# Opening order of a fused attention and MLP kernel: loads, normalization and small weights moved

## Chip, cores and metric

One core of one Trainium2 chip. The metric is the device time of one launch in microseconds, the median of several runs. The core has engines that run side by side, each with its own instruction stream in a fixed order: TensorE (PE, with weight loads shown as PEld), VectorE (DVE), ScalarE (ACT), GpSimd (POOL), and SyncE (SP), which here issues every DMA.

## What is computed

Sequence 2048, width 1024, 32 heads of 32, MLP width 3584, all in bf16.

```python
def reference(A_x, A_wqkv, A_wo, B_x, B_w1, B_b1, B_w2, B_b2):
    def _A_ref(x, wqkv, wo):
        qkv = (x @ wqkv).reshape(B, S, 3, H, Dh).transpose(2, 0, 3, 1, 4)
        q, k, v = qkv[0], qkv[1], qkv[2]
        scores = jnp.einsum("bhqd,bhkd->bhqk", q, k) * (Dh ** -0.5)
        o = jnp.einsum("bhqk,bhkd->bhqd", _softmax(scores, axis=-1), v)
        return o.transpose(0, 2, 1, 3).reshape(B, S, D) @ wo
    def _B_ref(x, w1, b1, w2, b2):
        y = _layernorm(x, axis=-1)
        return _gelu(y @ w1 + b1) @ w2 + b2
    x = A_x
    xn = _layernorm(x, axis=-1)
    s = _A_ref(xn, A_wqkv, A_wo)
    g = _silu(_B_ref(xn, B_w1, B_b1, B_w2, B_b2))
    return x + s * g
```

## The kernel before

x is cut into 16 tiles of 128 rows, t0 to t15. In the opening each tile is loaded, its mean and variance are taken (`bn_stats`, two halves of 512 columns on DVE; for t1 and t3 two activations with a running sum on ACT), the reciprocal root is made on POOL by a power, and DVE writes the normalized tile into one of four buffers `xnb` (L798). Then it is transposed into `xnT`: t0 to t3 and t5 by PE, with ACT copying the result out of PSUM (L786), the others by a DMA transpose on SP (L802), which waits for DVE.

Attention goes by head groups of four heads (eight groups), query blocks of 256 rows and pairs of key blocks. One *unit* is one head group, one query block, one block of 256 keys: eight score products on PE (L904), two exponentials of 128x1024 on ACT (L913). There are 512 units' worth of them. The K, Q and V projections of a head group must be there before its units; for the first group they are made in the opening, block by block (`k_item`, `q_item`, `v_half`), as tiles come in. K for blocks 0 to 2 is copied out of PSUM by ACT, from block 3 on by DVE. The first units go in the order `order0`: query blocks 0 and 1 on key blocks 0, 1, 2, ... with some of query block 2 between.

Between the scores PE does everything else: P times V, row sums, the projections of the next head group, and the MLP (W1 products in 112 items of 16, W2 products, L632). The W1 weights pass through three buffers `w1r`, the W2 weights through four `w2r`; in the opening the same memory holds exponentials of the first units, so the first W1 loads have to wait until these are used up. The MLP's input is x once more, normalized with another factor (`make_y`), transposed by DMA into `yT`.

In the last head group the output projection follows (L632 on `wo`, products of 512 columns): for the last query block seven of eight head groups can be summed ahead (`most`), and the eighth follows when the last quotient is there.

Who runs when is fixed when the program is built. A planner (`_Plan`) holds a list of operations with assumed durations (`occ`), latencies (`lat`), transfer rates and priorities (`prio`, smaller first), plays them through, and writes down one order for each engine. PE's items have positions and due units; `lead` is how many units ahead a due item gets precedence, `seeds` shake the positions in stretches of 30 us of the planner's time. `extra` names operations that a DMA must wait for beyond its data. So a changed constant can move instructions anywhere behind it. On the chip each engine goes through its order and waits at semaphores; nothing overtakes.

SP's order in the opening before: x0 to x3, wqk for K and Q, x4 to x11, the transpose of t4, x12, x13, wv, x14, x15, the other ten transposes, wqk for the next group's K, two loads of x for the MLP, b1, b2, wqk for its Q, two transposes for the MLP, then three W1 loads.

Of the kernel before, what the change touches and what calls it, by code (L numbers as in the profile page):

```python
# [8 lines left out]
BF16 = mybir.dt.bfloat16  # L9
# [23 lines left out]
class _Plan:  # L33
# [3 lines left out]
    def __init__(self):  # L37
        self.ops = []
        self.last_w = {}
        self.readers = {}  # L40
        self.s_queue = []
        self.pv_queue = []
        self.dense = {"pro": [], "q0": [], "v0": [], "tr": [], "last": [], "proj": [], "mlp": [], "w2": [], "wo": []}
        self.lead = 3
        self.filler, self.fill, self.fill0 = None, 0.6, 1400.0
        self.seeds, self.seg, self.amp, self.jit, self.w2b = (), 30000.0, 4.0, 0.1, 20.0
# [421 lines left out]
def bass_recurrent_scan__mha_block__mixer_channel_mlp__prompt_kernel(  # L468
# [27 lines left out]
        0, 0, 234914347, 0, 0, 0, 0, 0, 0, 0, 0, 0, 0, 0, 0, 0, 0, 0, 0, 0, 0, 0, 0, 0, 0, 0, 0, 0, 0,  # L496
# [3 lines left out]
    with ExitStack() as st:  # L500
# [28 lines left out]
        b1T = sb("b1T", [128, FB], BF16)  # L529
# [32 lines left out]
        xnb = [gw[:, i * 1024:(i + 1) * 1024] for i in range(4)]  # L562
        iota_i = utw[:].rearrange("p a b -> p (a b)")[:, 0:256].bitcast(I32)
# [19 lines left out]
        def c_b4(n):  # L583
            return 67 + 0.2605 * n
# [55 lines left out]
        def load_x(t, extra=()):  # L640
            dma(f"x{t}", lambda e: e.dma_start(xst[t], x2[t * 128:(t + 1) * 128, :]), 262144, [], [XS(t)],
                rate=390.0, prio=2, occ=500, lat=2450, extra=extra)
# [18 lines left out]
        for t in range(NTR, 12):  # L661
            load_x(t)
# [81 lines left out]
        def k_item(n):  # L744
            it = _Item("pro", 0.01 * n)
            for lo, w in ((0, 128), (128, 128)) if n < 2 else ((0, 256),):
                for dc in range(DC):
                    def fn(e, b, dc=dc, lo=lo, w=w):
                        at = n * 256 + lo
                        return mm(e, bank(b, lo, lo + w), wqk[wk0][:, dc, :], xnT[:, dc, at:at + w], dc == 0 and lo == 0, dc == DC - 1)  # L750
                    chunk(it, fn, Q256 if w == 256 else Q128, [("xnT", 2 * n + i, dc) for i in range(lo // 128, (lo + w) // 128)] + [("wqk", wk0)])
            if n >= 3:
                dve(lambda e: e.tensor_copy(QKT[0][:, 1, n * 256:(n + 1) * 256], bank(it.bank, 0, 256)), c_ps(256), [],
                    [("K", 0, n)], -1, it)
                return it
            act(lambda e: e.activation(QKT[0][:, 1, n * 256:(n + 1) * 256], bank(it.bank, 0, 256), ACT.Copy), c_act(256), [],
                [("K", 0, n)], -1, it)
            return it
# [35 lines left out]
        first = {}  # L794

        def normalize(t, rs):
            def nf(e):
                return e.tensor_scalar(xnb[t % 4], xst[t], mv[:, t, 0:1], lnp[:, t, 1:2], op0=ALU.subtract, op1=ALU.mult)  # L798
            rw = ([XS(t), ("mv", t), rs], [("xnb", t % 4)], 1)
            first[t] = pool(nf, 1150, *rw) if t in PN else dve(nf, c_b4(1024) + 118, *rw)  # L800
            if t >= NTR and t not in TRP:
                dma(f"tr{t}", lambda e: e.dma_start_transpose(xnT[:, :, t * 128:(t + 1) * 128], xnb[t % 4]), 262144,  # L802
                    [("xnb", t % 4)], [("xnT", t, c) for c in range(DC)], prio=0, rate=300.0, occ=1300, lat={4: 2800, 6: 2400, 7: 2000}.get(t, 1000))
# [10 lines left out]
        for n in range(NPR):  # L814
            if n == 6:
                for t in range(12, NT):
                    load_x(t, [first[4]])
                    if t == 13:
                        load_v(0, [first[4]])
            groups = [(2 * n,), (2 * n + 1,)] if n < 2 else [(2 * n, 2 * n + 1)]  # L820
            for ts in groups:
# [13 lines left out]
                for t in ts:  # L835
                    if t in AT:
                        continue
                    for c in range(2):
                        dve(lambda e, t=t, c=c: e.bn_stats(stats[:, t, c, :], xst[t][:, c * 512:(c + 1) * 512]),  # L839
                            605, [XS(t)], [("st", t, c)], 1.2)  # L840
# [4 lines left out]
                if ts[0] not in AT:  # L845
                    dve(lambda e, lo=lo, hi=hi: e.tensor_scalar_add(lnp[:, lo:hi, 0], mv[:, lo:hi, 1], EPS), 80,
# [22 lines left out]
        for n in range(NPR // 2):  # L869
            plan.dense["v0"].append(v_half(0, n, "pro", 0.2 + 0.01 * n))  # L870
            plan.dense["v0"][-1].hold = 6 + 2 * n

        rss = [("rs", t) for t in range(4)] + [("rs", 2 * n) for n in range(2, NPR)]
# [7 lines left out]
        dma("b1", lambda e: e.dma_start(b1T[:], B_b1.rearrange("(fb p) -> p fb", p=128)), 8192, [("s3",)], [("b1",)], lat=5500)  # L881
        dma("b2", lambda e: e.dma_start(b2b[:], B_b2.rearrange("(o d) -> o d", o=1).to_broadcast([128, D])), 262144,
            [("s3",)], [("b2",)], occ=2900)
# [139 lines left out]
        def proj(hg, w):  # L1023
            wk = load_qk(hg, 1, [first[NT - 1]] if hg == 1 else ())
            wq = load_qk(hg, 0)
# [26 lines left out]
        def load_w1(p):  # L1052
            gi, pi = p % NW1R, p % NW1
            src = B_w1[:, pi * 256:(pi + 1) * 256].rearrange("(c p) f -> p c f", p=128)
            dma(f"w1{gi}", lambda e: e.dma_start(w1r[:, gi], src), 524288, [], [("w1", gi)], lat=3100.0)
# [9 lines left out]
        def make_y(c):  # L1065
            for t2 in range(2):
                t = 2 * c + t2
                dma(f"yx{t2}", lambda e, t=t, t2=t2: e.dma_start(yst_t[t2][:], x2[t * 128:(t + 1) * 128, :]), 262144, [],
                    [("yst", t2)], rate=390.0, extra=[w1_ev[4]] if c == 1 else ())
# [118 lines left out]
        def mlp(u0, u1):  # L1188
# [4 lines left out]
            for s_ in seq:  # L1193
# [5 lines left out]
                if s_[0] == "w1":  # L1199
                    load_w1(s_[1] * NW1 + s_[2])  # L1200
                    it = w1_item(s_[1], s_[2])
                else:
# [364 lines left out]
```

## Time and profile before

| | us |
|---|---|
| three runs | 1029.39, 1031.92, 1032.52 (median 1031.92) |
| the profiled execution | 1031.42 |
| its span in the profile | 1029.6 |
| ACT busy | 1016.6 |
| PE busy | 1004.2 |
| DVE busy | 956.8 |
| ACT idle in 0 to 50 us, all of it | 6.1 |
| ACT idle from 50 to 1000 us | 0.3 |
| ACT idle in the last 29.6 us | 6.6 |

The span is the profile's own clock, from the first to the last event; the profiled execution's time is 1.8 us more. PE's busy time counts overlapping matmuls by modelled ends and says little about how near PE is to its peak. The granted TensorE clock is full (1.00 in every window, 0.96 in the last). An engine's idle row names the engine or DMA whose event ended it.

### The profile page before, as it was taken

To read this page: it belongs to the slowest core of one execution; us is meant where nothing else is said; L and a number is where in the kernel's file an instruction comes from. 1 tells how busy PE (TensorE), PEld (TensorE's weight loads), DVE (VectorE), ACT (ScalarE), POOL (GpSimd) and SP (SyncE) were. 2 spreads that over 40 slices of the span, in tenths; PEclk is the share of its full clock that TensorE was granted. 3 is DMA by queue.
4 is the path that set the end of the run, shared out by engine and by line. 5 is a ranking of instruction groups with operands and counts; after the bars stand their busy time and mean duration, and the time that the engine had idled before them with its cause. 6 is when DMAs were issued, how large, how long until landed. Compare 5 with 4: busy or idle time off the path is not lost.

```text
span 1029.6 us, 31985 instructions
## 1 busy us (share of the span) xinstructions
PE 1004.2 (98%) x14355; PEld 635.9 (62%) x14355; DVE 956.8 (93%) x1365; ACT 1016.6 (99%) x1087; POOL 11.8 (1%) x21
## 2 busy tenths in 40 slices
PE   8999999999999999999999999999999999999997
PEld 7566656666766576666665676665666665564443
DVE  8899999899899998998899999998999889978987
ACT  8999999999999999999999999999999999999997
POOL 2200000000000000000000000000000000000000
PEclk9999999999999999999999999999999999999999
DMA  8867845745764767446556575556355753873331
GB/s 221 153 154 201 206 123 167 207 110 136 206 187 129 196 189 201 129 134 195 142 146 190 154 215 159 158 173 174 88 150 166 218 161 88 274 230 120 108 93 64
DMA packets 317146, 167.77 MB, mean 163 GB/s; under 512 B 55632, under 2 KB 304976, under 8 KB 317008
## 3 DMA queue, kind: packets, MB, share of 16 engines
q1 hardware_dynamic: 317008, 165.71, 58.2%
q8 instruction: 113, 1.85, 0.8%
q14 instruction: 25, 0.20, 0.1%
HBM read 146.55 MB, written 12.06 MB: 154 GB/s over the span
## 4 chain that ended last, share of the span: by engine, by line
ACT 78%; PE 10%; DVE 7%; DMA 4%; issue 1%; POOL 0%; SPq 0%
ACT P L913 71%; PE ps L632 7%; ACT ut L1127 4%; DMA w2r<-in_B_w_dram 3%; PE ps L904 2%; DVE stats L839 1%; PE ps L627 1%; ACT P L1248 1%; DVE PA L930 1%; ACT gw L1155 1%; DVE PR L944 1%; DMA xnT<-gw 1%; DVE gw L798 1%; ACT w2r L913 1%; DMA hT<-in_A_x_dram 0%
## 5 line engine op out<-in xcount | busy, mean ns | idle before, releaser
L913 ACT ACTIVATE P<-ps 128x1024 bf16<-128x1024 f32 x988 | 921.3, 1228 | 0.8 <-PE ps L904 0.7
L930 DVE TENSOR_TENSOR PA<-P 128x2048 bf16<-128x2048 bf16 x173 | 210.0, 1217 | 28.4 <-ACT P L913 27.7
L632 PE MATMUL ps<-yT,w1r 128*128 128x256 bf16 x1792 | 227.7, 273 | 0.4 <-DVE QKT L730 0.3
L632 PE MATMUL ps<-w2r,hT 128*128 128x256 bf16 x1792 | 223.8, 273 | 2.0 <-DMA w2r<-in_B_w_dram 1.2
L944 DVE TENSOR_TENSOR PR<-PR,PA 128x2048 bf16<-128x2048 bf16 x173 | 209.7, 1213 | 1.4
L904 PE MATMUL ps<-QKT 32*128 32x256 bf16 x4032 | 200.2, 273 | 8.7 <-ACT P L913 6.2
L632 PEld LDWEIGHTS ps<-yT,w1r 128*128 128x128 bf16 x1792 | 163.8, 98 | 53.1 <-issue 29.1
L632 PEld LDWEIGHTS ps<-w2r,hT 128*128 128x128 bf16 x1792 | 163.0, 98 | 52.4 <-issue 30.6
L904 PEld LDWEIGHTS ps<-QKT 32*128 32x128 bf16 x4032 | 59.7, 92 | 138.2 <-ACT P L913 130.0
L627 PE MATMUL ps<-P,V 128*32 128x256 bf16 (+1 forms) x4080 | 137.6, 272 | 0.0
L632 PE MATMUL ps<-xnT,wqk 128*128 128x512 bf16 (+2 forms) x584 | 132.2, 354 | 2.4 <-DMA xnT<-gw 1.0
L627 PEld LDWEIGHTS ps<-P,V 128*32 128x32 bf16 x4080 | 95.3, 96 | 33.2 <-issue 24.0
L632 PE MATMUL ps<-wv,xnT 128*128 128x256 bf16 (+2 forms) x704 | 87.8, 264 | 1.6 <-DMA xnT<-gw 1.0
L632 PEld LDWEIGHTS ps<-xnT,wqk 128*128 128x128 bf16 x584 | 49.9, 98 | 51.7 <-issue 15.2
L1096 DVE TENSOR_TENSOR hT<-ps,b1T 128x512 bf16<-128x512 f32 x112 | 76.8, 685 | 4.4 <-PE ps L632 4.0
L930 DVE TENSOR_TENSOR PR<-P 128x2048 bf16<-128x2048 bf16 x60 | 72.8, 1214 | 0.0
L632 PEld LDWEIGHTS ps<-wv,xnT 128*128 128x128 bf16 x704 | 55.8, 98 | 23.9 <-issue 10.8
L1127 ACT ACTIVATE ut<-ut 128x3072 bf16<-128x3072 bf16 (+2 forms) x27 | 59.6, 2206 | 0.0
L730 DVE CAST QKT<-ps 128x512 bf16<-128x512 f32 x58 | 39.7, 685 | 1.5 <-PE ps L632 1.1
L999 DVE STREAM_TRANSPOSE nt<-ps 128x256 f32<-128x256 f32 x63 | 27.9, 444 | 14.0 <-PE ps L627 13.9
L1121 DVE TENSOR_TENSOR ut<-hT 128x2048 bf16<-128x2048 bf16 (+1 forms) x37 | 35.3, 957 | 0.1
L1130 DVE TENSOR_TENSOR hT<-ut,hT 128x2048 bf16<-128x2048 bf16 (+1 forms) x37 | 35.0, 951 | 0.0
(116 smaller groups left out, 587.8 us busy)
## 6 DMA issues: line engine op xcount, KB each, us to landing
w1r<-in_B_w_dram SPq DMA_DIRECT2D x112, 512.0 KB, 4.4
w2r<-in_B_w_dram SPq DMA_DIRECT2D x128, 448.0 KB, 4.5
yst<-in_A_x_dram SPq DMA_DIRECT2D x18, 256.0 KB, 4.5
wqk<-in_A_wqkv_dram SPq DMA_DIRECT2D x16, 256.0 KB, 3.7
g_scratch<-gw SPq DMA_DIRECT2D x32, 128.0 KB, 3.3
hT<-in_A_x_dram SPq DMA_DIRECT2D x14, 256.0 KB, 3.9
o_scratch<-ot SPq DMA_DIRECT2D x56, 64.0 KB, 3.4
xnT<-o_scratch SPq DMA_DIRECT2D x7, 512.0 KB, 6.4
```

The costliest lines, as they stand in the source:

```text
L627: ins = e.matmul(dst(j), lhsT=lhsT(j), rhs=rhs(j), start=start, stop=stop, tile_position=(0, 32 * j), skip_group_check=True)
L632: return e.matmul(dst, lhsT=lhsT, rhs=rhs, start=start, stop=stop, skip_group_check=True)
L730: dve(lambda e: e.tensor_copy(QKT[sl][:, which, tq * 512:(tq + 1) * 512], bank(it.bank)), c_ps(512), [], [(nm, sl, 2 * tq), (nm, sl, 2 * t ...
L904: ins = e.matmul(bank(b0[j], kk * 256, (kk + 1) * 256), lhsT=QKT[sl][32 * j:32 * j + 32, 1, kb * 128:(kb + 1) * 128], rhs=QKT[sl][32 * j:3 ...
L913: x = act(lambda e, h=h: e.activation(Pt[pi][:, 2 * h:2 * h + 2].rearrange("p j k q -> p (j k q)"), ps[:, pr[h] * 1024:(pr[h] + 1) * 1024] ...
L930: return dve(lambda e: e.tensor_tensor(dst[:].rearrange("p u j q -> p (u j) q"), src[:].rearrange("p u j k q -> p (u j) k q")[:, :, 0, :], ...
L944: return dve(lambda e: e.tensor_tensor(fl3(pr), fl3(pr), fl3(PA[i]), op=ALU.add), c_b16(2048), [("PA", i), tok], [tok], 3.2)
L999: dve(lambda e: e.transpose(nt_t[:], bank(pv.bank, 256, 512)), c_ps(256) + 120, [], [("nt",)], prio, pv)
L1096: w1_ev[p] = dve(lambda e: e.tensor_tensor(hT[:, hs], bank(it.bank).rearrange("p (k t) -> p k t", k=2), b1T[:, 2 * pi:2 * pi + 2].unsqueez ...
L1121: dve(lambda e, u_=u_, x_=x_: e.tensor_tensor(u_, x_, x_, op=ALU.mult), c_b16(n), hs_, [("ut", ui)], gp)
L1127: act(lambda e: e.activation(ua, ua, ACT.Tanh, scale=GC), c_acts(run * 512), uts, uts, ga)
L1130: dve(lambda e, u_=u_, x_=x_: e.tensor_tensor(x_, u_, x_, op=ALU.mult), c_b16(n), [("ut", ui)] + hs_, hs_, gp)
```

## The change

- x loads: wv now goes out between x9 and x10. x12 and x13 wait for t4's normalization, x14 and x15 for t7's (before, all four and wv stood behind t4's).
- b1 is no longer loaded transposed in one DMA of single elements, but as four DMAs of 28 rows of 32 values into the tail of `ut`, early in the queue; GpSimd clears the place first, and DVE transposes it into `b1T` after the last normalization.
- K's third block is copied by DVE and not by ACT (`n >= 2`).
- The normalizations of t0 to t3 get precedence over statistics (priority 0.8 for 1).
- Later loads get conditions: wqk for the next group's K after t15's transpose, its Q after an exponential of the third query block, W1 loads 1 and 2 after such exponentials, the first x load for the MLP after t15's transpose, b2 after the fifth W1 item, wqk of group 2 after the third.
- Planner constants: `lead` 5 for 3, the one nonzero seed is 0, some assumed rates and durations. They issue nothing themselves, but move the order: in ACT's stream the first 12 and the last 101 of 1085 instructions stay in place, in PE's the first 55 and the last 3 of some 14,360.

```diff
-        self.lead = 3
+        self.lead = 5
...
-        0, 0, 234914347, 0, 0, 0, 0, 0, 0, 0, 0, 0, 0, 0, 0, 0, 0, 0, 0, 0, 0, 0, 0, 0, 0, 0, 0, 0, 0,
+        0, 0, 0, 0, 0, 0, 0, 0, 0, 0, 0, 0, 0, 0, 0, 0, 0, 0, 0, 0, 0, 0, 0, 0, 0, 0, 0, 0, 0,
...
-        b1T = sb("b1T", [128, FB], BF16)
+        b1T = sb("b1T", [128, 32], BF16)
...
+        b1c = utw[:, 7, 480:512]
...
-        for t in range(NTR, 12):
-            load_x(t)
+        load_x(4)
...
+        load_x(9)
+        load_v(0)
+        load_x(10)
+        load_x(11)
+        pool(lambda e: e.memset(b1c, 0.0), 150, [], [("b1c", k) for k in range(4)], 0)
+        for k in range(4):
+            dma(f"b1{k}", lambda e, k=k: e.dma_start(b1c[32 * k:32 * k + FB, :], B_b1.rearrange("(q b p) -> b q p", b=4, p=32)[k]),
+                2048, [], [("b1c", k)], prio=2)
...
-            if n >= 3:
+            if n >= 2:
                 dve(lambda e: e.tensor_copy(QKT[0][:, 1, n * 256:(n + 1) * 256], bank(it.bank, 0, 256)), c_ps(256), [],
...
-            rw = ([XS(t), ("mv", t), rs], [("xnb", t % 4)], 1)
+            rw = ([XS(t), ("mv", t), rs], [("xnb", t % 4)], 0.8 if t < NTR else 1)
...
-            if n == 6:
-                for t in range(12, NT):
-                    load_x(t, [first[4]])
-                    if t == 13:
-                        load_v(0, [first[4]])
+            if n == 3:
+                load_x(12, [first[4]])
+                load_x(13, [first[4]])
+            if n == 4:
+                load_x(14, [first[7]])
+                load_x(15, [first[7]])
...
+        dve(lambda e: e.transpose(b1T[:], b1c), c_b16(32) + 60, [("b1c", k) for k in range(4)], [("b1",), ("ut", 1)], 2.5, None, [first[NT - 1]])
...
-        dma("b1", lambda e: e.dma_start(b1T[:], B_b1.rearrange("(fb p) -> p fb", p=128)), 8192, [("s3",)], [("b1",)], lat=5500)
-        dma("b2", lambda e: e.dma_start(b2b[:], B_b2.rearrange("(o d) -> o d", o=1).to_broadcast([128, D])), 262144,
-            [("s3",)], [("b2",)], occ=2900)
...
-            wk = load_qk(hg, 1, [first[NT - 1]] if hg == 1 else ())
-            wq = load_qk(hg, 0)
+            wk = load_qk(hg, 1, [trs[NT - 1]] if hg == 1 else [w1_ev[2]] if hg == 2 else ())
+            wq = load_qk(hg, 0, [got[(2, 7)][0]] if hg == 1 else ())
...
-                    [("yst", t2)], rate=390.0, extra=[w1_ev[4]] if c == 1 else ())
+                    [("yst", t2)], rate=390.0, extra=[w1_ev[4]] if c == 1 else [trs[NT - 1]] if c == 0 else ())
...
-                    load_w1(s_[1] * NW1 + s_[2])
+                    load_w1(s_[1] * NW1 + s_[2], [got[(2, 5)][0]] if s_[1] == 0 and s_[2] == 1 else [got[(2, 7)][0]] if s_[1] == 0 and s_[2] == 2 else ())
                     it = w1_item(s_[1], s_[2])
+                    if s_[1:] == (0, 4):
+                        dma("b2", lambda e: e.dma_start(b2b[:], B_b2.rearrange("(o d) -> o d", o=1).to_broadcast([128, D])), 262144,
+                            [], [("b2",)], occ=2900, extra=[w1_ev[4]])
```

The order of SP in the opening after: x0 to x3, wqk for K and Q, x4 to x9, wv, x10, x11, the four b1 pieces, the transpose of t4, x12, x13, the transposes of t6 and t7, x14, x15, the other eight, wqk for the next group's K, two loads and two transposes for the MLP, the first W1 load, a store of the attention's output, W1 load 1, wqk for the next group's Q, W1 load 2. On ACT, the first half unit's exponential now stands before the copy of tile 3 and not behind it. In the tail of PE, 14 products of 512 columns stand between the last P times V and the last two products; before, these two follow directly.

## The prediction

> **What bounds the kernel now.** I read the page's engine line first, then the list of what ScalarE (ACT) waited for, then the timeline of the first 60 us and of the last 30, and the chain of waits between them.
>
> ```profile
> PE 1004.2 (98%) x14355; PEld 635.9 (62%) x14355; DVE 956.8 (93%) x1365; ACT 1016.6 (99%) x1087; POOL 11.8 (1%) x21
> ...
> L913 ACT ACTIVATE P<-ps 128x1024 bf16<-128x1024 f32 x988 | 921.3, 1228 | 0.8 <-PE ps L904 0.7
> ```
>
> ACT is busy 1016.6 of 1029.6 us, nearly all of it on the exponentials of L913. One shows 1228 ns, but they overlap: 921.3 us over 988 is 0.93 us each. All that this change can win is in ACT's 13.0 idle us and in what it takes off ACT. The waits:
>
> ```profile
> ACT PR L1480 <- PE ps L632: 3.0, 1, 3.0
> ACT PA L825 <- DMA hT<-in_A_x_dram: 2.5, 2, 2.0
> ACT w1r L913 <- PE ps L904: 1.2, 1, 1.2
> ACT QKT L913 <- PE ps L904: 0.8, 1, 0.8
> ACT L667 <- PEq L1552: 0.7, 1, 0.7
> ACT P L913 <- PE ps L904: 0.7, 2, 0.5
> ACT xnT L786 <- PE ps L782: 0.4, 1, 0.4
> ```
>
> The first line is the tail, the second the arrival of x0 and x3. Between, ACT starts its first exponential at 13.46 and then stands three times: 0.51 at 22.36, 0.76 at 28.53, 1.18 at 44.24. From 45.42 on it is packed; in the windows from 50 to 1000 us it lacks 0.29 us in all. The three stands in the timeline:
>
> ```profile
> 21.85 0.51 ACT L756 ACTIVATE QKT<-ps 128x256 bf16<-128x256 f32 x1
> 22.87 3.77 ACT L913 ACTIVATE P<-ps 128x1024 bf16<-128x1024 f32 x4 [0.51 <-PE ps L904]
> 27.86 1.05 PE L632 MATMUL ps<-xnT,wqk 128*128 128x256 bf16 x8 [0.82 <-DMA xnT<-gw]
> 29.29 1.94 ACT L913 ACTIVATE QKT<-ps 128x1024 bf16<-128x1024 f32 x2 [0.76 <-PE ps L904]
> 43.63 0.62 PE L632 MATMUL ps<-wv,xnT 128*128 128x128 bf16 x8 [0.65 <-DMA xnT<-gw]
> 44.59 0.45 PE L632 MATMUL ps<-wv,xnT 128*128 128x128 bf16 x5 [0.34 <-DMA xnT<-gw]
> 45.42 3.77 ACT w1r L913 x4
> ```
>
> (The last line is from the chain of waits; after the start and the duration, square brackets give the idle time before the row and what ended it.) The reader sees that PE is in order: scores that have their data stand behind a K or V product that waits for a transposed tile. Those tiles are late because of DMA. By the landing times of L802, t4's transpose lands 2.9 us after its issue, t10 to t13 2.7 to 2.8, but t6 and t7, issued behind wv, x14 and x15 (those take 6.9 to 7.2), 6.0 and 4.5, and t14 and t15, with wqk and two yst loads right behind them, 5.5 and 5.1.
>
> **The change, part by part.** Sums are against the profiled execution: span 1029.6, time 1031.42, so 1.8 us lie outside the span; it is 0.5 under the median 1031.92.
>
> *K2 on VectorE.* The copy of K's third block (L756) leaves ACT. It ends 0.28 after the exponential before it (22.36 against 22.08): -0.28. The scores waited for it, and in the new order DVE makes the copy while PE runs six Q2 products: -0.51. DVE pays a 128x256 cast (0.42 us, L740's row) early, but Q3's cast moves behind the last normalization, so the count before that is equal.
>
> *wv, x12 to x15.* wv is issued at about 9.1, behind x9. The table of windows shows 356 GB/s at 8 to 12 us and 11 GB/s at 14 to 16: there is a hole that 0.5 MB fills in about 1.6 us. x10 and x11 come that much later; their statistics start at 21.36, so it is hidden by some 5 us. x14 and x15 are now issued behind t6 and t7 (about 23.5); with their worst landing, 7.2, they are there at 30.7, and DVE reads them at 30.9 now, about 32 in the new order; bare cover, 0 to +0.3, I take 0. With wv, x14 and x15 out of the way t6 and t7 should land about 2.9 after issue, t7 near 25.0 instead of 27.8. Then K3 doesn't wait: -0.76.
>
> *wqk, yst and b2 later.* wqk2 waits for t15's landing, so t14 and t15 land 2.8 after issue. DVE's own chain is about 0.4 shorter at the last normalization (38.5 against 38.88: its wait of 1.18 at K3 goes, but V's third cast now stands in front of t14's normalization and follows the pace of ACT). t15 is there at about 41.8 against 44.54. In the new order the scores of the sixteenth unit stand behind the V products of t14 and t15; these end at 42.3, ACT asks at 43.6: -1.18. b2 moves behind the fifth W1 product and is first read by a W2 product; with 6.4 us to land it is hidden.
>
> *b1 in four DMAs.* Four issues of at most 0.43 us each, after x11 (10.4 to 12.2); SP has nothing else until t4's transpose at 15.2. The new transpose on DVE is a 128x32 piece after the last normalization: 0.15 to 0.3 us (rows of small DVE operations, 128x8 to 128x128), off the chain. The memset on GpSimd takes 0.1 of the 5 us before the first transpose on PE.
>
> Where the old b1 load, 2-byte runs, took 6.2 us to land, four of that kind would be in at 12.2 + 6.2 = 18.4, t4's transpose behind them at 21.3, and K2, due at 20.6, would wait 0.7. The new rows are whole runs of 64 B, so I take 0 and keep +0.7 as the bound. The Trainium skill, "DMA: Bandwidth & Descriptors", section Specifications, says that transfers under 512 B are not moved at line rate and cost a read-modify-write, which speaks against these rows too; by it the sum would be up to 0.7 higher.
>
> *Normalization in front of statistics, and the new start.* t1 is normalized 0.24 sooner, but ACT, which copies the transposed tiles out, is full from x3's arrival (6.89) to 12.15, so nothing comes of it. Q0's cast goes ahead of one statistics step: 11.9 instead of 12.34, and the first exponential at about 12.8 instead of 13.46. But in ACT's new order the copy of tile 3 comes after this first half unit, no longer before it. K1 hangs on it: tile 3 copied 13.75 to 14.7, its eight products to 15.3, K1's copy to 15.9, scores, next exponential 16.4, where the one before ended at 15.6. So ACT waits 0.62 + 0.5, and about 0.2 for tile 5, where now it waits 0.39: +0.95. Bounds: 0 (nothing late) and +1.5 (another late pair).
>
> *The steady part.* W1 loads 1 and 2 wait for exponentials, a store of the attention's output stands between them in SP's queue, and the first W1 product moves from behind unit 25 to unit 29. PE's work between the scores (128x512 at 0.216 us, 128x256 at 0.109, 128x128 at 0.058, a 32-row product at a quarter, as the products' rows step) is 43.8 us in the first 32 units against 48.3, is 10.9 behind at unit 192, and has caught up to 2.6 at unit 512. Between neighbouring scores it is at most 4.1, beside a tanh of 2.64, as it is now (4.2). ACT waits stay at the 0.3 shown: 0, with bounds -0.3 and +4.5 (five stands of the 0.5 to 1.2 kind).
>
> *The tail.* Here is what the backlog costs. Now the last products are two on the last head group (L632), after
>
> ```profile
> 1024.75 0.60 PE L632 MATMUL ps<-yst,xnT 128*128 128x512 bf16 x2 [1.58 <-DVE xnT L1282]
> 1025.39 0.60 ACT L1480 ACTIVATE PR<-ps 128x512 bf16<-128x512 f32 x1 [3.03 <-PE ps L632]
> ```
>
> a wait of 1.58 for the quotient. In the new order 14 products of 512 columns (two output pieces, seven head groups each), done earlier before, stand between the last P.V and these two: 14 x 0.215 = 3.0, of which the wait hides 1.58. On DVE three steps (L1472's, L1475's and one L1492) fall behind the quotient; at 0.6 a step its chain ends 1.5 later too. +1.5. Bounds: +1.0 (one step fits into a gap) and +2.6 (the second seven wait for a bank until the first is read).
>
> Sum: -0.28 - 0.51 - 0.76 - 1.18 + 0.95 + 0 + 1.5 = -0.3. Span 1029.3, time **1031.1**. Own range 1029.5 to 1033.
>
> **The rivals.**
>
> *The gain stays whole.* The start doesn't stand (0 for +0.95) and the tail's 14 products fit (0 for +1.5): -2.73, 1028.7. For it: each pause is under a microsecond and worked from neighbouring rows. Against: both orders are fixed at the build, and the tail's chain has one hole of 1.58 only.
>
> *Slower: scores stand behind W1 and W2 products in the steady part.* The loads come later, the same three W1 buffers have to make up 11 us of PE work between units 192 and 512, and each product whose weights are late holds the scores behind it. For it: PE does wait for w2r now (1.2 us, three times), and ACT has no slack to give it back. Against: making up 11 us over 320 units is 0.03 a unit, where PE waits for ACT 0.2 to 0.4 in most units of the timeline. It decides from about four stands of 0.9; with five, +4.5: 1035.6.
>
> *The transposes land no sooner.* t6 and t7 meet x12 and x13 instead of wv, t14 and t15 are slow by themselves. Then 0.76 and 1.18 stay: 1031.1 + 1.94 = 1033.0. For it: x12 and x13 are issued 16.6 to 17.6 and took 3.7 to 5.8 here. Against: t10 to t13, alone, took 2.8. The Trainium skill, same page, section Queues, rings and completion order, says that a completion count lands only after every earlier write of that DMA engine; the 6.0 behind wv agrees, and by that rule t6 is clean once x12 and x13 are in.
>
> **How the numbers follow.** Forecast 0.36, transposes no sooner 0.14 (both within 0.3% of the median, that is 1028.8 to 1035.0, about what a measurement here can tell from no change), gain whole 0.27, steady part slower 0.23. So faster 0.27, same 0.50, slower 0.23. The range takes the gain whole with the steady 0.3 and half a microsecond more, and the five stands: 1027.8 to 1035.6.
>
> **What would show it.** ACT: no wait near 22 and 44, none at the scores behind K3; no L756 for the third K block; the first exponential near 12.8, with a wait near 16. SP: t6, t7, t14, t15 landing under 3.5 us. ACT's sixteenth unit near 43.7. The tail: PE's last two products with no wait for the quotient, 14 others right before, and ACT's idle before its copy to PR at 4.5 (3.0 now). I am wrong in direction if ACT's wait from 50 to 1000 us exceeds 3 us, or if the tail is no longer than now.

## The result and the profile after

| | before | after |
|---|---|---|
| median of six runs each, us | 1030.74 | 1036.64 |
| lowest to highest | 1029.34 to 1032.52 | 1035.50 to 1040.99 |
| profiled execution, and its span | 1031.42, 1029.6 | 1040.99, 1039.1 |
| ACT busy | 1016.6 | 1017.2 |

By the medians the change makes the kernel 5.9 us slower. The ratio is estimated from all the runs and is not the quotient of the medians: 1.0065 with a 95% interval from 1.0053 to 1.0078, that is 6.7 us (5.5 to 8.0). Differences in us below are of medians, and good to about 1 us. The forecast was 1031.1; the result lies 1.0 above the upper end of its range. The profiled execution of after is the longest of its six, so some losses in its lines are larger than in the median run, and one of them, the stand at 32 us, is missing in other traces of the same opening, as the experiments show.

The engine line and two groups of the page of after:

```profile
PE 1004.7 (97%) x14360; PEld 637.9 (61%) x14360; DVE 956.2 (92%) x1367; ACT 1017.2 (98%) x1086; POOL 11.9 (1%) x22
...
L633 PE MATMUL ps<-w2r,hT 128*128 128x256 bf16 x1792 | 224.7, 274 | 4.2 <-DMA w2r<-in_B_w_dram 3.7
...
L924 ACT ACTIVATE P<-ps 128x1024 bf16<-128x1024 f32 x988 | 921.2, 1216 | 6.1 <-PE ps L915 5.8
```

Line numbers have moved: the exponentials are L924 (before L913), the scores L915, the general product L633, the DMA transposes L814. The exponentials cost what they did, 921.2 us. What is new is idle time: 6.1 us before exponentials into `P` (0.8 before) and 3.7 us of PE waiting for W2 weights (1.2). ACT's waits, from the table of waits of after (total, times, longest):

```profile
ACT P L924 <- PE ps L915: 5.8, 7, 2.2
ACT PR L1494 <- PE ps L633: 5.6, 1, 5.6
ACT w1r L924 <- PE ps L915: 3.5, 2, 2.4
ACT PA L838 <- DMA hT<-in_A_x_dram: 2.3, 2, 2.0
ACT L679 <- PEq L1566: 0.7, 1, 0.7
```

The lines for `QKT` at 22 and 28 us are gone, as predicted. In their place the opening has stands at 32 and 46 us, the steady part has some, and the tail's wait is 5.6 instead of 3.0. The first new stand, in the timeline of after:

```profile
31.49 1.05 PE L633 MATMUL ps<-xnT,wqk 128*128 128x256 bf16 x8 [1.33 <-DMA xnT<-gw]
...
32.92 1.02 ACT L924 ACTIVATE P<-ps 128x1024 bf16<-128x1024 f32 x1 [0.96 <-PE ps L915]
```

PE waits 1.33 us for t8 and t9, which K's fifth block needs, and ACT stands 0.96 behind it. The second, thirteen microseconds on, in the same view:

```profile
44.88 0.93 PE L633 MATMUL ps<-wv,xnT 128*128 128x128 bf16 x7 [2.60 <-DMA xnT<-gw]
...
46.37 2.34 PE L633 MATMUL ps<-xnT,wqk 128*128 128x256 bf16 x10
46.41 1.94 ACT L924 ACTIVATE w1r<-ps 128x1024 bf16<-128x1024 f32 x2 [2.38 <-PE ps L915]
...
49.46 1.02 ACT L924 ACTIVATE w1r<-ps 128x1024 bf16<-128x1024 f32 x1 [1.12 <-PE ps L915]
```

V's products for t14 and t15 wait 2.60 for t15's transpose, with the scores queued behind them. Then ten K and Q products take 2.34 us, where eight took 1.05 at 31.49. The table of windows says why (the length, busy times of PE, PEld, DVE, ACT and POOL, then granted clock, DMA share, GB/s):

```profile
38.00:40.00 2.00, 1.45 (x28) 1.00 (x24) 1.97 (x5) 2.00 (x3) 1.83 (x3) 1.00 0.35 80
40.00:42.00 2.00, 0.67 (x14) 0.47 (x15) 2.00 (x4) 2.00 (x4) 1.92 (x2) 1.00 1.67 124
42.00:44.00 2.00, 0.28 (x5) 0.10 (x2) 2.00 (x4) 2.00 (x3) 0.18 (x1) 0.74 0.34 70
44.00:46.00 2.00, 1.12 (x15) 0.80 (x15) 0.45 (x1) 0.02 (x1) 0.00 (x0) 0.50 0.03 7
46.00:48.00 2.00, 2.00 (x17) 1.26 (x10) 0.69 (x1) 1.59 (x2) 0.00 (x0) 0.50 1.02 289
48.00:50.00 2.00, 1.91 (x17) 0.81 (x16) 1.62 (x3) 0.88 (x2) 0.00 (x0) 0.55 0.27 98
```

PE is busy 0.95 us from 40 to 44, and from about 43 on the granted clock is half, until nearly 50 (0.55 in the last row); before, it was 1.00 in all of this stretch. So the wait is followed by slow products, and these bring the third stand, 1.12. The Trainium skill, "TensorE: Matmul & The Clock Gate", section What's actually happening, says that the clock falls to half after an idle window of about 3.4 us. The trace agrees with the half rate; but PE was not idle for a whole 3.4 us, only 2.60 of it at a stretch.

The transposes themselves, by the rows of L814 (issue time, and the microseconds from issue to landing): one query for t8 and t9, one for t14 and t15. Of two landing times the least is the first tile's and the most the second's.

```profile
L814 SPq DMA_TRANSPOSE xnT<-gw x2: 1237/1604/1972, 24.6 to 25.9; - x2
DMA to landing us min/median/max: 4.4/4.9/5.5
...
L814 SPq DMA_TRANSPOSE xnT<-gw x2: 1232/1270/1307, 38.2 to 39.5; - x2
DMA to landing us min/median/max: 2.7/4.0/5.3
```

t8 takes 4.4 and t9 5.5: x14 and x15 are now issued right ahead of them, at 23.54. t14 takes 2.7, as forecast, but t15 5.3, with nothing issued behind it until it had landed (wqk follows at 44.85). t6 and t7, whose delay the change was to end, take 2.7 and 2.8 (6.0 and 4.5 before).

In the steady part the largest stand is in the last W2 group (timeline of after):

```profile
902.81 2.27 PE L633 MATMUL ps<-w2r,hT 128*128 128x256 bf16 x11 [1.63 <-DMA w2r<-in_B_w_dram]
...
905.67 1.94 ACT L924 ACTIVATE P<-ps 128x1024 bf16<-128x1024 f32 x2 [2.19 <-PE ps L915]
```

The last W2 products have moved from behind unit 458 to behind unit 461. Five of their weight loads are now issued from 887.9 to 899.7, in between the 512 KB reads of the attention's output, and land after 7.4 to 12.0 us; before, the twelve issued from 880.8 to 909.6 took 5.8 in the median and 9.4 at most. The late weights are not all of it: PE is busy only 0.71 us from 899.71 to 903.12, and the granted clock is half from there to 906.54, so the eleven products above take 2.27 us.

The tail, in the timeline of after:

```profile
1030.87 0.29 PE L628 MATMUL ps<-P,ones 128*32 128x128 bf16 x6 [0.95 <-issue]
1031.10 0.60 PE L633 MATMUL ps<-V,xnT 128*128 128x512 bf16 x2
1031.54 0.81 PE L633 MATMUL ps<-wqk,xnT 128*128 128x512 bf16 x3
1032.18 0.59 PE L633 MATMUL ps<-wv,xnT 128*128 128x512 bf16 x2
1032.62 0.59 PE L633 MATMUL ps<-V,xnT 128*128 128x512 bf16 x2
1033.05 0.81 PE L633 MATMUL ps<-wqk,xnT 128*128 128x512 bf16 x3
1033.69 0.59 PE L633 MATMUL ps<-wv,xnT 128*128 128x512 bf16 x2
1034.13 0.59 PE L633 MATMUL ps<-yst,xnT 128*128 128x512 bf16 x2
```

These are the fourteen products of the prediction and the two last, without any wait for the quotient. In front of them PE stood 0.95 us for nothing that the profile shows.

### The profile page after: what moved, and what is told of

It reads as the page before. It is cut to its first block, busy times and chain, and to the rows that moved or that the text cites. A ratio compares the mean times of both kernels' runs of the same rounds, so it can differ in the third digit from the quotient of the medians.

```text
span 1039.1 us, 32004 instructions
## 1 busy us (share of the span) xinstructions
PE 1004.7 (97%) x14360; PEld 637.9 (61%) x14360; DVE 956.2 (92%) x1367; ACT 1017.2 (98%) x1086; POOL 11.9 (1%) x22
## 4 chain that ended last, share of the span: by engine, by line
ACT 79%; PE 14%; DMA 5%; DVE 1%; issue 0%; SPq 0%; POOL 0%; DVEq 0%
ACT P L924 72%; PE ps L633 10%; DMA w2r<-in_B_w_dram 4%; ACT ut L1138 3%; PE ps L915 2%; PE ps L628 2%; ACT gw L1166 1%; ACT P L1262 1%; DMA xnT<-gw 1%; ACT w2r L924 1%; ACT xnT L798 0%; DMA hT<-in_A_x_dram 0%; DVE stats L852 0%; ACT PA L838 0%; ACT w1r L924 0%
## 5 line engine op out<-in xcount | busy, mean ns | idle before, releaser
L924 ACT ACTIVATE P<-ps 128x1024 bf16<-128x1024 f32 x988 | 921.2, 1216 | 6.1 <-PE ps L915 5.8
L633 PE MATMUL ps<-w2r,hT 128*128 128x256 bf16 x1792 | 224.7, 274 | 4.2 <-DMA w2r<-in_B_w_dram 3.7
L633 PE MATMUL ps<-yT,w1r 128*128 128x256 bf16 x1792 | 227.0, 273 | 0.9 <-DVE hT L1107 0.6
L915 PE MATMUL ps<-QKT 32*128 32x256 bf16 x4032 | 200.8, 273 | 13.7 <-ACT P L924 9.6
L633 PEld LDWEIGHTS ps<-w2r,hT 128*128 128x128 bf16 x1792 | 163.7, 98 | 55.5 <-issue 30.4
L633 PEld LDWEIGHTS ps<-yT,w1r 128*128 128x128 bf16 x1792 | 164.2, 98 | 52.0 <-issue 28.3
L915 PEld LDWEIGHTS ps<-QKT 32*128 32x128 bf16 x4032 | 59.8, 92 | 143.4 <-ACT P L924 132.0
L628 PE MATMUL ps<-P,V 128*32 128x256 bf16 (+1 forms) x4080 | 137.0, 272 | 0.9 <-ACT P L924 0.9
L633 PE MATMUL ps<-xnT,wqk 128*128 128x512 bf16 (+2 forms) x584 | 132.0, 357 | 2.7 <-DMA xnT<-gw 1.3
L628 PEld LDWEIGHTS ps<-P,V 128*32 128x32 bf16 x4080 | 95.6, 96 | 32.3 <-issue 22.8
L633 PE MATMUL ps<-wv,xnT 128*128 128x256 bf16 (+2 forms) x704 | 87.7, 265 | 2.6 <-DMA xnT<-gw 2.6
L633 PEld LDWEIGHTS ps<-xnT,wqk 128*128 128x128 bf16 x584 | 50.2, 98 | 53.2 <-issue 15.2
L633 PEld LDWEIGHTS ps<-wv,xnT 128*128 128x128 bf16 x704 | 56.0, 98 | 25.8 <-issue 11.0
L1134 DVE TENSOR_TENSOR ut<-ut,hT 128x2048 bf16<-128x2048 bf16 (+1 forms) x37 | 35.2, 951 | 0.0
```

The costliest lines, as they stand in the source:

```text
L628: ins = e.matmul(dst(j), lhsT=lhsT(j), rhs=rhs(j), start=start, stop=stop, tile_position=(0, 32 * j), skip_group_check=True)
L633: return e.matmul(dst, lhsT=lhsT, rhs=rhs, start=start, stop=stop, skip_group_check=True)
L915: ins = e.matmul(bank(b0[j], kk * 256, (kk + 1) * 256), lhsT=QKT[sl][32 * j:32 * j + 32, 1, kb * 128:(kb + 1) * 128], rhs=QKT[sl][32 * j:3 ...
L924: x = act(lambda e, h=h: e.activation(Pt[pi][:, 2 * h:2 * h + 2].rearrange("p j k q -> p (j k q)"), ps[:, pr[h] * 1024:(pr[h] + 1) * 1024] ...
L1134: dve(lambda e, u_=u_, x_=x_: e.tensor_tensor(u_, u_, x_, op=ALU.mult), c_b16(n), [("ut", ui)] + hs_, [("ut", ui)], gp)
```

## The experiments

The first question is which of the three places costs how much, the second why t15 is late. Each kernel is the changed one with a small edit, unless it says otherwise. Each batch had its own runs of the kernel before (medians 1030.11 to 1030.93), to which the ratios refer.

**V's last quarter behind later scores.** V's products for tiles 12 to 15 are held back until 17 units have their scores, instead of 12. (The expectations speak of V2 and V3 in places; it is this one item, V's products of four tiles.) The planner then also returns to the order before for the later W1 and W2 products and for the tail.

```diff
-            plan.dense["v0"][-1].hold = 6 + 2 * n
+            plan.dense["v0"][-1].hold = 6 + 2 * n if n < 3 else 17
```

> The changed kernel, with the V product of tiles 12 to 15 held back until 17 units' scores are out (hold 17 for 12). Theory (scores stand in PE's queue behind a V product that waits for the transpose of tile 15): ACT's wait of 2.38 us before the sixteenth unit and the 1.12 us after it go, and PE's granted clock stays at 1.00 between 40 and 50 us, though the transpose of tile 15 still lands about 5 us after its issue. In this build the order also has its fourteenth W1 item behind unit 54 as before (59 in the change) and no product of the output projection between the last P times V and the last two; so ACT's idle before its copy to PR is 3.0 to 3.6 and not 5.6. Time: 1036.6 less 3.5 less 1.6 to 2.6, so 1030.5 to 1031.5. Rival (the transposes themselves are the limit, whoever stands behind them): the wait moves to the first units on the eighth key block and the total falls by less than 1.5, to 1035 or more in the opening's share; ACT shows a wait of 2 us or more between 44 and 52.

1032.47 us, ratio 1.0019 (1.0010 to 1.0029): 4.2 under the changed kernel, and 1 above the upper expectation. The timeline of this kernel shows why it isn't all:

```profile
43.33 0.60 PE L633 MATMUL ps<-xnT,wqk 128*128 128x256 bf16 x4 [2.06 <-DVE PR L1317]
...
44.31 1.94 ACT L924 ACTIVATE w1r<-ps 128x1024 bf16<-128x1024 f32 x2 [1.52 <-PE ps L915]
...
47.41 1.94 ACT L924 ACTIVATE w1r<-ps 128x1024 bf16<-128x1024 f32 x2 [1.16 <-PE ps L915]
```

K7, which needs t14 and t15 as well, now stands in front of the same scores. The row names a DVE step as the releaser, but t15's transpose lands at 43.2, just before the products start. The clock from 40 to 50 us is 0.83. So the wait has only changed its product. The tail's wait is 3.9, more than expected, because PE stood 0.96 us for nothing shown in front of the last row sums, as in the trace of after. Whether the loss is mostly t15 or mostly the later order, this run can't tell, since the edit changed both.

**Instruction counts shifted.** In the raw DMA records a group of 15 to 21 packets of a transpose hangs for 1 to 3 us at a time, and a fetch of instructions usually starts just before (113 of 16 KB in the run, about one for 256 PE instructions if a product and its weight load count as two, and 25 of 8 KB). The two clocks are matched only roughly. Times in us, for the opening:

```
kernel             packets hang      fetch starts    transpose
before             23.27 - 26.06     22.98           t6 lands after 6.0
before             41.46 - 43.72     40.12, 41.94    t14, t15: 5.5, 5.1
after              41.42 - 43.41     40.97           t15: 5.3
V's last later     40.01 - 41.81     39.59           t15: 5.2
```

To move the fetches, PE's idle loop in the first 7 us got 122 filler products of 40 columns instead of 46 of 128, so that every later instruction lies 76 products, with their weight loads 152 instructions, further on.

```diff
-            for _ in range(n):
-                ins = e.matmul(bank(b, 0, 128), lhsT=ident[:], rhs=ident[:], start=True, stop=True, skip_group_check=True)
+            for k in range(3 if n == 1 else n):
+                w = 40 if n == 1 else 128
+                ins = e.matmul(bank(b, 0, w), lhsT=ident[:], rhs=ident[:, 0:w], start=True, stop=True, skip_group_check=True)
```

> The changed kernel in the same order; each filler matmul of the first 6 us is cut into three of 40 columns, 76 matmuls more, so that every later 16 KB instruction fetch (one per 256 instructions of PE's stream) comes 152 instructions sooner: the one that began at 40.97 us at about 34. Theory (DMA transposes stand still for some 2 us when an instruction fetch starts while they run): tile 15's transpose lands 2.7 to 2.9 us after issue instead of 5.3, ACT's wait before the sixteenth unit falls from 2.38 to under 0.5, the 1.12 behind it shrinks with it, and a stall may turn up at another transpose where a fetch now falls (tiles 12 and 13). Time 1033 to 1034. Rival (tile 15's transpose is slow for a reason of its own place, such as GpSimd's power of 128x16 that runs beside it, or the MLP's loads): it lands at 5.3 as before, and the time stays at 1036 to 1037.

1033.88, ratio 1.0034 (1.0021 to 1.0046), 2.8 under the changed kernel. The hangs moved to 17.5, 24.5 and 33.6, each within 0.9 us after a fetch; t15 landed after 3.5, and ACT's stands at `w1r` shrank from 3.5 to 1.5. GpSimd's power of 128x16, which the expectation names as a rival, still runs beside t15 (37.83 to 40.88). So in this one trace the hangs moved with the instruction stream; that the fetch itself holds the packets up is the likely reading, not more.

**x14 and x15 behind t9's transpose.** Only SP's order changes.

```diff
-            if n == 4:
-                load_x(14, [first[7]])
-                load_x(15, [first[7]])
+            if n == 5:
+                load_x(14, [first[9]])
+                load_x(15, [first[9]])
```

> The changed kernel, x14 and x15 issued behind the transposes of tiles 8 and 9 and not before them; every other engine's order is the same. Theory (the loads of x14 and x15 hold up what is issued right behind them): the transposes of tiles 8 and 9 land 2.7 to 3.0 us after issue (4.4 and 5.5 now), PE's wait of 1.33 before the fifth K block and ACT's wait of 0.96 near 32 us go, unless the statistics of tile 14 then wait for their load. Gain at most 1.0 at that place; and since the transpose of tile 15 sets the sixteenth unit, the gain may be lost there, so the time is 1035.6 to 1036.6. Rival (tile 9 is late for an instruction fetch at 29.5): it lands at 5 us or more all the same.

1037.45, ratio 1.0070 (1.0058 to 1.0082): no gain. t8 and t9 land after 2.7 and 2.8 and ACT does not stand at 32 us; t15 lands after 5.3, and ACT stands there 2.2 and 0.7. The collision is real: in the four traces of kernels that issue x14 and x15 right ahead (after, V's last quarter later, the shifted instructions, and the other later order below) t8 and t9 take 3.5 to 5.5 us, in the seven that don't 2.7 to 2.8. But only after itself, the longest of its runs, has the stand. In the other three t8 and t9 take at most 4.0 and ACT doesn't stand there. In the timeline of the kernel with the other later order K's fifth block has no wait in front of it:

```profile
30.27 1.04 PE L633 MATMUL ps<-xnT,wqk 128*128 128x256 bf16 x8
```

So in a usual run there is nothing at 32 us for this move to win. Where the stand does occur, it is not only its own 0.96: the later normalizations shift as well, and t15's transpose is issued at 39.48, against 38.09 here.

**The tail alone, in the kernel before.** The two sums ahead of the last query block are held to the end; 14 products of 512 columns come behind the last P.V, and all else up to there is as before.

```diff
+                            if fin and i2 >= 2:
+                                most.hold = 64 * HG
```

> The kernel before, with one edit: the seven-head-group sums of the last two output pieces may start only when all scores are out. PE's order is the same for 13,976 of 14,357 instructions and ends as in the change: 14 products of 512 columns between the last P times V and the last two. Theory: the tail's price is 14 x 0.215 = 3.0 less the hole of 1.58, so +1.5 to +1.7, a time of 1032.2 to 1032.5 against 1030.74, and ACT's idle before its copy to PR 4.5 to 4.7 for 3.0. Rival (the tail costs the whole 2.6 by which that idle grew): 1033.3 or more. Second rival (it was hidden or is an accident of the profiled run): within 0.5 of 1030.74.

1032.80, ratio 1.0026 (1.0015 to 1.0037): 1.9 us by the medians (2.7 by the ratio, 1.5 to 3.8), ACT's wait 4.7. The term of the prediction was +1.5, the wait 4.5.

**Both moves together.** V's last quarter and x14, x15 as above.

> The two earlier moves together: V2 and V3 behind later scores, and the x14 and x15 loads issued behind t9's transpose. Theory A (the opening is set by the moment t15's transpose lands, whatever ACT does before): the 0.96 us stand at the fifth K block goes, t8 and t9 land in 2.7 to 2.9, ACT reaches the scores behind K7 0.9 us sooner and stands there 0.9 us longer; time as with V2 and V3 moved alone, 1032.2 to 1032.8. Theory B (each stand is a term of its own, as the sum of the prediction has it): 1031.3 to 1031.7.

1032.20, ratio 1.0018 (1.0008 to 1.0028), beside 1.0019 with V alone: theory A's time. t8 and t9 are clean, K7 starts at 43.80 after a wait of 2.08, ACT stands 1.55 there. But the trace of V alone has no stand at the fifth K block either, so there was no 0.96 to move, ACT does not stand 0.9 longer, and this run doesn't tell the two theories apart. It does show what the clock is worth: it stays full here, and the second stand, 1.16 with V alone, is gone. (The tail's wait is 4.3; PE stood 1.32 for nothing shown in front of the last row sums.)

**K7 later too.** The planner is told a truer landing of t15; it puts K7 behind the scores of the eighteenth unit, V's last quarter and seven groups of P.V and row-sum products.

```diff
-                    ..., lat={4: 3000, 6: 1600}.get(t, 1000))
+                    ..., lat={4: 3000, 6: 1600, 15: 4000}.get(t, 1000))
```

> As the run before, and the planner is told that t15's transpose lands 4 us after its issue slot, so that K7 stands behind the scores of the seventeenth and eighteenth units, with filler products in PE's hole. Theory A (the scores need only wait for t15 because K7 stands in front of them; two units, 3.9 us of exponentials, lie between): the stands of w1r's exponentials (1.5 and 1.2 us with V2 and V3 moved alone) go or stay under 0.5, PE's granted clock from 40 to 50 us is 0.95 or more, and the time is 1029.3 to 1030.3, below the kernel before. Theory B (ACT then waits as long two units later, at the scores that need K7): a stand of 1.5 or more near 48 us, 1031.8 to 1032.8.

1032.47, ratio 1.0016 (1.0007 to 1.0024): theory B's time and its place of the wait, but not its cause. The timeline of this kernel:

```profile
47.67 1.05 PE L633 MATMUL ps<-xnT,wqk 128*128 128x256 bf16 x8
...
50.07 2.86 ACT L924 ACTIVATE w2r<-ps 128x1024 bf16<-128x1024 f32 x3 [2.17 <-PE ps L915]
```

t15 is there at 42.8, and no product waits for it. K7 starts at 47.67 only because it stands too far back; its copy on DVE ends at 49.6, behind two sums, and the scores follow. The later order has moved too, and the tail's wait is 3.7.

**K7 right behind the seventeenth unit, V's last quarter behind the eighteenth.** The latency 3400 in place of 4000, the hold 18 in place of 17; later order and tail as before.

> As the run with K7 later, but K7 stands right behind the seventeenth unit's scores and V2 and V3 behind the eighteenth's; the order of the later W1 and W2 products and the three products of the tail are those of the kernel before. Theory A (the opening loses only where K7's or V's products stand ahead of scores that could run): no stand of w1r or w2r exponentials over 0.5 us, PE's granted clock 0.95 or more from 40 to 50 us, time 1029.0 to 1030.7. Theory B (t15's landing itself is too late for K7 wherever it stands): a stand of 1 us or more between 44 and 50 us and 1031.5 to 1032.5.

1031.73, ratio 1.0016 (1.0007 to 1.0025). Behind the start's waits ACT has no stand until 58 us; there it stands 2.68 (and once more at 201 us, 1.06). Its scores were issued three microseconds before:

```profile
55.06 0.40 PE L915 MATMUL ps<-QKT 32*128 32x256 bf16 x8
...
58.45 1.94 ACT L924 ACTIVATE P<-ps 128x1024 bf16<-128x1024 f32 x2 [2.68 <-PE ps L628]
```

What ended the wait is a P.V product (L628), not a score: the exponential writes into a place of `P` that, it seems, the P.V products before 58 us had not yet read. Neither theory foresaw this. t15 is no longer the reason; PE had waited 0.89 us at 54.74 for DVE's cast of V, so V, now one unit later, and P times V behind it are the likely ones, and the next run bears it out.

**The same with the hold at 17.**

> The same opening, except that V2 and V3 may follow one unit earlier. That alone makes the planner put the last W1 and W2 products as late as in the changed kernel (behind units 433 and 463, against 431 and 459), with 25 products behind the last P.V (17 in the changed kernel, 3 before). Theory A (the late order costs by itself, in the tail and at the W2 loads): ACT's wait before its copy to PR 5 to 6.5 us, one to three waits of PE for w2r between 60 and 1000 us, and 2 to 4 us more than the run before this one. Theory B (it is the opening's stands that cost, the late order is harmless but for the tail): no w2r wait over 0.5, and 1.5 to 2.5 us more.

The opening is the quietest so far: no stand from 17 to 60 us. And the time is 1035.38, ratio 1.0040 (1.0028 to 1.0053). ACT's two largest lines in the table of waits:

```profile
ACT PR L1494 <- PE ps L633: 6.0, 1, 6.0
ACT P L924 <- PE ps L915: 3.0, 5, 1.2
```

1.1 of the 3.0 lie in the start, 1.9 in stands at 136, 519 and 697 us. PE waits for w2r 0.6 in all; the largest, 1.25 at 519, is at scores that waited for a cast of Q (0.23) behind projection products. So the late order costs, but not only at the W2 loads: theory A named the right size and too narrow a cause.

**The changed kernel with another later order.** One number of the planner's noise is set, for 90 to 120 us; all engines' instructions are those of the changed kernel up to about 90 us, and the tail has 3 products again. (3, 17 and 25 are the planner's counts; the traces show 2, 16 and 24 products of 512 columns behind the last P.V.)

```diff
-        0, 0, 0, 0, 0, 0, 0, ...
+        0, 0, 0, 267418254, 0, 0, 0, ...
```

> The changed kernel with one number of the planner's noise set for 90 to 120 us: every engine's instructions are those of the changed kernel up to about 90 us, and from there W1 and W2 products are in another order, with 3 products behind the last P.V instead of 17. Theory A (the opening of the changed kernel costs about 2.2 us, the late order the rest): stands at 32, 46 and 49 us as in the changed kernel, no wait of PE for w2r over 0.6 us from 60 us on, ACT's wait before its copy to PR 3.0 to 4.0, time 1032.0 to 1033.3. Theory B (the loss is made in the opening, the later waits would come with any order): 1034.5 or more.

1033.62, ratio 1.0036 (1.0023 to 1.0048), 0.3 above theory A's range. The table of waits of this kernel:

```profile
ACT w1r L924 <- PE ps L915: 3.6, 2, 2.6
ACT PR L1494 <- PE ps L633: 3.0, 1, 3.0
ACT PA L838 <- DMA hT<-in_A_x_dram: 2.8, 1, 2.8
ACT P L924 <- PE ps L915: 1.5, 4, 0.6
```

The stands at t15 are as in the changed kernel (2.65 and 0.91), the one at 32 us, which theory A also expected, is not there; from 60 to 1000 us ACT waits 0.44. So of the 5.9 us about 3.0 belong to the opening and 3.0 (1036.64 less 1033.62) to the later order; by the ratios it is 3.7 and 3.0. The run also shows what gains ahead of t15 are worth: ACT asks for the sixteenth unit's scores at 43.24, 1.0 us sooner than in the kernel before (44.24), and gets them at 45.89, 0.5 later (45.42).

**The quiet opening with the same order, and with a third one.** The kernel of the backlog run, with the same number of the noise; and with another number for 150 to 180 us.

> The kernel of the backlog run (opening without stands from 17 to 60 us) with the same number in the planner's noise for 90 to 120 us: the later order of the run beside it, 3 products behind the last P.V. Theory A (opening and late order are separate terms): 3 us off the tail and 1.9 off the steady waits of the backlog run's profile, span 1028.7, time 1029.0 to 1030.3. Theory B (what the opening gains is lost later whatever the order): 1031.5 or more.

> The same opening with another number for 150 to 180 us: 14 more products than the run before in the whole, again 3 behind the last P.V. Theory A: 1029.0 to 1030.5, within 0.7 of the run before. Theory B: 1031.5 or more.

1028.65, ratio 0.9984 (0.9975 to 0.9993), and 1029.13, ratio 0.9988 (0.9979 to 0.9997): both faster than before, by 1.9 and 1.4 us in the medians. The table of waits of the first:

```profile
ACT PR L1494 <- PE ps L633: 3.0, 1, 3.0
ACT PA L838 <- DMA hT<-in_A_x_dram: 1.8, 1, 1.8
ACT P L924 <- PE ps L915: 1.1, 2, 0.6
ACT L679 <- PEq L1566: 0.7, 1, 0.7
ACT xnT L798 <- PE ps L794: 0.4, 1, 0.4
```

From 20 to 1000 us ACT has no wait that the table lists. t15 still takes 5.4 us to land here; nothing that could run stands behind it. No run moves K7 and V in the kernel before, so how much of this gain would come without the change is not known.

## Why the prediction was wrong

| term | predicted | in the trace of after |
|---|---|---|
| K2's copy off ACT | -0.28 | done by DVE |
| stand at 22.36 | -0.51 | gone |
| K3's stand (t6, t7) | -0.76 | gone; 2.7 and 2.8 to land, 2.9 predicted |
| new start | +0.95 | +0.5 (ACT idle 4.1 up to 17 us, for 3.6): first exponential at 12.63 (12.8 predicted), waits of 0.59 and 0.50 |
| t8, t9 | not in the sum | +0.96, in this trace only |
| t14, t15 | -1.18 | +2.3: stands of 2.38 and 1.12 for the 1.18 before |
| steady part | 0 | +3.5 (3.7 for 0.2 in the tables of waits); +3.7 (4.0 for 0.3) by the windows from 50 to 1000 us |
| tail | +1.5 | +2.6 (5.6 for 3.0) |

**The step that failed first** is "wqk2 waits for t15's landing, so t14 and t15 land 2.8 after issue". t14 does, t15 takes 5.3. The prediction saw two slow transposes with loads behind them and took the loads for the cause, since t10 to t13, alone, took 2.8. The raw records had another: a hang that is tied to the place in the instruction stream. In the changed kernel and the nine variants whose early stream lies where it was, t15 took 4.7 to 5.8, though no wqk or yst load follows it; in the one with the stream shifted, 3.5. The rival "transposes land no sooner" named it ("t14 and t15 are slow by themselves") but priced it at the old wait of 1.18. The 6.0 of t6, which the prediction puts down to wv, x14 and x15 in front of it, has a hang in it too (23.27 to 26.06), so that row can't tell the two causes apart.

**Why it was larger than that wait.** In the new order V's products of t14 and t15 stand in front of the sixteenth unit's scores, and the opening came earlier to the same landing: by ACT's start of the first exponential into `w2r` (51.28 against 49.05) the opening is 2.2 us behind, where the sum had it 1.8 ahead. PE's idle time also halved the clock, and with it came the stand of 1.12 that no term held; in the kernel with both moves, where the clock stayed full, there is no such stand. x14 and x15 in front of t8's and t9's transposes were looked at only for their own landing, not for what they do to the transposes behind them; that costs a stand in the trace of after and none in three others with the same order of SP.

**The steady part** was put at 0, with five stands as the other bound, because the same PE work has to be made up over 320 units. An average is the wrong quantity: what counts is where single products meet late data. The kernel with the quiet opening and the late order has 1.9 us of such stands, the changed kernel's opening with the other order 0.44. By the profiled execution the changed kernel has 3.7, above the 3 us that were named as the sign of a wrong direction; in the other two kernels with its order, the shifted instructions and the moved x loads, it is 1.4 and 2.7. The rival "slower" had the mechanism in part (in after PE waits 0.91, 0.54 and 1.63 us for W2 weights right ahead of the three largest stands; in the quiet opening with the late order the largest is behind a cast of Q), and left opening and tail as forecast. Its size, +4.5, fits the profiled execution only.

**The tail** was right in its mechanism: the 14 products come where they were said to, PE has no wait for the quotient, and in the kernel where it is the only change ACT waits 4.7 (4.5 predicted), which costs 1.9. In the other two kernels with this tail the wait is 4.4 and 5.0. The 5.6 of the profiled execution are about these 4.7 and the 0.95 in which PE stood for nothing shown, in front of the last row sums. With 25 products the wait is 6.0.

**Where the 5.9 us went**: by the runs 3.0 in the opening and 3.0 in the later order, of which the tail by itself is 1.9. The rest, about 1, would be the steady part of a median run; no run measures it alone, and by the tail's interval (1.5 to 3.8) it may be nothing. That the late order came out of the early constants was luck, bad here: one number of the planner's noise gives another. With t15 off the path of other scores, an order without the backlog, and x14 and x15 behind t9, the change's loads go with 1.9 us less than before; whether the loads or the moved K and V bring that, no run shows.

## What to carry to other kernels

On an engine with a fixed order, ask of each product what stands behind it that could run without its data: moving K and V of the late tiles behind one and two more units of scores took the stand away, which neither cleaner queues nor another place of the hang had done. Gains ahead of a wait on an absolute arrival are not terms of a sum. And where a planner writes the order, compare late order and tail before and after any early edit: here the early edits moved 3 us there, and one number of the planner's noise took them back.

## What the hardware showed that was not expected

A 256 KB DMA transpose within the chip's memory lands 2.7 to 2.9 us after its issue when undisturbed, and 4.2 to 6.1 when its packets hang. The hang takes 1 to 3 us, mostly hits 15 to 21 packets at once, and in most cases starts within 0.9 us after an instruction fetch; shifting PE's stream by 76 products moved it from 41 us to 17, 24 and 34 us. In three of the kernels a hang starts 0.4 to 0.6 us ahead of the nearest fetch by the roughly matched clocks, so the order of cause is not settled.

How PE's granted clock goes down is not a matter of the single wait. With both moves together, PE waits 2.08 us for t15 and the clock stays full (the table of windows of that kernel):

```profile
40.00:42.00 2.00, 1.72 (x14) 0.43 (x12) 2.00 (x5) 2.00 (x4) 1.22 (x2) 1.00 1.34 46
42.00:44.00 2.00, 0.20 (x2) 0.22 (x3) 1.57 (x2) 1.23 (x2) 0.00 (x0) 1.00 0.30 67
44.00:46.00 2.00, 2.00 (x20) 0.92 (x18) 0.69 (x2) 1.22 (x2) 0.00 (x0) 1.00 0.61 140
```

PE is busy 1.92 of these first 4 us. With V alone moved it is busy 1.94 in the same 4 us, with a wait of 2.06, and the clock is 0.59 in the 2 us after; with the instructions shifted it has no wait over 1.30 but is busy 1.94 from 38 to 42, and the clock is half from 42 to 48. So the clock can fall without any wait near 3.4 us, and a stretch of some 4 us at half load can also pass.

What decides is how the stretch lies. In all thirteen traces the times between two changes of the clock are whole multiples of 3.413 us (in after: full for 37.547, half for 6.827, full for 853.332, half for 3.413), counted from the moment, 4.2 to 7.2 us into the span, when it first became full, which differs from run to run. Cut into these steps, up to 1010 us:

| kernel | step | PE busy in it, us | clock in the next step |
|---|---|---|---|
| after | 899.71 to 903.12 | 0.71 | half |
| x14 and x15 behind t9 | 39.63 to 43.05 | 0.95 | half |
| after | 39.55 to 42.97 | 1.29 | half |
| V's last quarter later | 40.93 to 44.35 | 1.36 | half |
| instructions shifted | 37.90 to 41.32 | 1.74 | half |
| both moves | 40.00 to 43.41 | 1.72 | full |
| x14 and x15 behind t9 | 892.97 to 896.38 | 1.79 | full |

The other three falls follow 1.28 to 1.54 us, and no other step at full clock has less than 2.0. So by these traces the limit lies near half of a step, 1.7 us, and the two cases around it can't be told apart by modelled busy times. The clock came back after half-clock steps with 2.99 us or more of work, and not after those with 0.55, 1.50 and 2.81.
